# Setting places in each engine's order for the operand steps of the second MLP, and moving three conversion pieces and the last norm

## The chip, the cores and the metric

The kernel runs on one core of a Trainium2 chip. The metric is the device time of one execution in microseconds (us); the median of three runs is used. Engines: TensorE (PE; PEld is its weight load), VectorE (DVE), ScalarE (ACT), GpSimd (POOL) and SyncE (SP), whose queue issues the DMAs.

## The reference

```python
attn_out = _attn_ref(q, k, v)          # 4 x 8 heads, 576 tokens, head size 64: scores * decay mask, @ v
x = attn_out.transpose(0, 2, 1, 3).reshape(2304, 512)
h = x @ w_in                           # 512 -> 2048
x = (h * np.cos(h)) @ w_out            # 2048 -> 512
rms = np.sqrt(np.mean(x * x, axis=-1, keepdims=True) + 1e-06)
xn = x / rms * rms_g
g = xn @ w_gate                        # 512 -> 1536
out = (g / (1 + np.exp(-g)) * (xn @ w_val)) @ w_out   # 1536 -> 512
```

All inputs are float32. The kernel splits operands into a high part and a remainder (`hi`, `lo`) and makes each product of three matmuls: hi·hi, hi·lo, lo·hi.

## The kernel before, in words

**Tokens.** `xall` holds the 2304 tokens (features on the partitions, four chunks of 128). The first MLP goes over five token tiles in the order `ORDER_A = [0, 1, 2, 4, 3]`: four of 512 tokens, and tile 4, of 256, as the fourth. The second MLP goes over three groups of 768 tokens, each as two halves of 384.

**First MLP (stage one).** There are 80 steps `i`, 16 per tile: steps 0 to 15 are tile 0, 48 to 63 the short tile 4, 64 to 79 tile 3, the last. A step makes one block of 128 hidden features (`hidden`, L176 to L178, 12 matmuls into a PSUM tile `g`, of which there are three), then `gate_cos`: ScalarE rounds (L386), VectorE subtracts (L387), ScalarE takes the sine (L389), VectorE multiplies (L393), ScalarE casts to `ghi` (L395), and VectorE or GpSimd makes `glo` (`minus`, L113). Three steps later (`LAG`) `out_t` multiplies the result with the output weights into four accumulators (12 matmuls). At a tile's end ScalarE copies the accumulators to `xall` (L572) and `norm` puts the tile's RMS norm on a list, `background`: four squares, `total` (a cast and a GpSimd `minus`), two pauses, `mean` (two matmuls with ones), two pauses, `guess` (two operations), nine Newton operations, four scales, and a note that the tile is normal: 25 entries. `idle()` takes one entry off; a step calls it once, from step 64 on three times.

The weights of the second MLP are converted beside this in 36 pieces. `piece_steps` weaves one piece into a step's gate: an absolute value on ScalarE, two operations on VectorE, then a cast and a subtraction of the piece before (for output weights only), and three more operations. `begins` lists the steps that begin one: 15 in each of tiles 1 and 2, and six in the short tile, at 48, 50, 53, 56, 58 and 61 (`LAST_BEGINS = (0, 2, 5)`, modulo 8). In steps that begin one, `glo` is made on VectorE, in others on GpSimd.

From step 67 on, `ahead(n)` makes the operands of group 0 one place per step (L522 casts, L526 differences t1 to t4), then, at n = 8 and 10, all of `quad_steps(0)` and `quad_steps(1)`, and fetches three blocks of output weights.

**Second MLP (stage two).** A quad is a pair of weight blocks times one group: seven products (L688, six matmuls of 384 columns each) in two PSUM tiles `alpha` and `beta` from the ring `h` (two slots), combined by ScalarE copies `s` (L695) and VectorE additions (L708, L715, L716) into four results r11, r22, r12, r21. In even quads a result passes through Silu (L710); in odd ones it is multiplied with it and split again (`shi`, `slo`). Between the products stand `fill` matmuls of the output product (L664, nine at a time). There are 12 quads per group, n = 0 to 35. In group 0 `quad_steps(q + 1)` makes the next quad's operands: `step0` (`plain`: a cast L479 and a subtraction), `step1` (four operations on `z`, L483 to L486), `step2` (two casts L491, two subtractions, then two stores by SyncE and the fetch of later values); groups 1 and 2 fetch what was stored. `operand_steps(g + 1)` makes the seven operands of the next group during quads 8 to 11. Three hooks in a quad call these: after r11, before r22's second part, and after r21.

**What sets the order.** From step 16 on ScalarE, VectorE and GpSimd run in the order of the code (`manual_schedule`); in stage two TensorE as well. In stage one TensorE's order is set by the framework's planner.

Of the kernel before, what the change touches and what calls it, by code (L numbers as in the profile page):

```python
# [30 lines left out]
P = 128  # L31
# [33 lines left out]
LAG = 3  # L65
LAST_BEGINS = (0, 2, 5)
MANUAL = NF1
# [8 lines left out]
def body(ctx: ExitStack, tc, qkv, qkr, vr, w1, w2, rg, gq, gk, mask, out):  # L76
# [230 lines left out]
    def norm(t):  # L307
# [20 lines left out]

        def pause():
            pass  # L330

        def mean():
# [26 lines left out]
        background.append(total)  # L359
        background.extend([pause, pause, mean, pause, pause, guess])  # L360
        background.extend([lambda s=s: newton(s) for _ in range(3) for s in range(3)])
        background.extend([lambda kc=kc: scale(kc) for kc in range(KC)])
        background.append(lambda: normal.append(t))

    def idle():
        if background:
            background.pop(0)()

# [75 lines left out]
    begins = [i for i in range(NF1, 3 * NF1) if (i + 1) % NF1]  # L444
    begins += [i for i in range(3 * NF1, 4 * NF1) if i % 8 in LAST_BEGINS]

# [26 lines left out]
    def quad_steps(q):  # L473

        plain, sums = side(q)
        z = values_of.pop(q)

        def step0():
            nc.scalar.copy(plain[:, 0], z[:, :3])  # L479
            minus(nc.vector, plain[:, 1], plain[:, 0], z[:, :3])  # L480

        def step1():
            nc.vector.tensor_tensor(z[:, 4], z[:, 0], z[:, 3], op=ALU.subtract)  # L483
            nc.vector.tensor_tensor(z[:, 3], z[:, 3], z[:, 2], op=ALU.add)
            nc.vector.tensor_tensor(z[:, 0], z[:, 3], z[:, 0], op=ALU.subtract)
            nc.vector.tensor_tensor(z[:, 1], z[:, 1], z[:, 0], op=ALU.subtract)  # L486

        def step2():
            for n in (0, 2):
                src = z[:, n + n // 2:n + n // 2 + 2]  # L490
                nc.scalar.copy(sums[:, 0, n:n + 2], src)  # L491
                minus(nc.vector, sums[:, 1, n:n + 2], sums[:, 0, n:n + 2], src)
# [5 lines left out]
        return [step0, step1, step2]  # L498

# [11 lines left out]
    def operand_steps(g):  # L511

        x = lambda a, b: xall[:, 2 * a:2 * a + 2, g * GROUP + b * HALF:g * GROUP + (b + 1) * HALF]

        def place(k):
            t = places.pop(0) if g else slot()
            ops[g, k] = t, t[:, 0, :, :HALF], t[:, 1, :, :HALF]
            return ops[g, k][1:]

        def split(k, src):  # L520
            hi, lo = place(k)
            nc.scalar.copy(hi, src)  # L522
            minus(nc.vector, lo, hi, src)

        def minus_to(dst, a, b):
            nc.vector.tensor_tensor(dst, a, b, op=ALU.subtract)  # L526

        def t24():
            minus_to(x(1, 1), x(1, 1), x(0, 0))
            split(2, x(1, 1))  # L530
            minus_to(x(1, 0), x(1, 0), x(1, 1))

        def t13():
            minus_to(x(0, 0), x(0, 1), x(0, 0))
            minus_to(x(0, 1), x(1, 1), x(0, 1))

        return [lambda: split(0, x(0, 0)), lambda: split(1, x(1, 0)), t13, lambda: split(5, x(1, 1)), t24,
                lambda: split(3, x(0, 1)), lambda: split(4, x(0, 0)), lambda: split(6, x(1, 0))]

    def ahead(n):  # L540

        if n == 0:
            late["steps"] = operand_steps(0)
        while late["steps"] and len(slots) == n:
            late["steps"].pop(0)()
        if 7 <= n < 11:
            slot()
            if n % 2 == 0:
                a, b = (t.rearrange("p a b c -> p (a b c)") for t in slots[-2:])
                sides.append((a[:, :6 * 2 * P].rearrange("p (h n c) -> p h n c", h=2, n=3),  # L550
                              b.rearrange("p (h n c) -> p h n c", h=2, n=4)))
                for step in quad_steps(len(sides) - 1):
                    step()
        elif n >= 11:
            fetch_out(n - 11)
# [23 lines left out]
    for i in range(LAST + LAG):  # L579
# [28 lines left out]
        if first:  # L608
            while converted[0] < min(len(blocks1), i + CONV_LEAD + 1):
                blocks1[converted[0]].convert(temps())  # L610
                converted[0] += 1
        idle()
        if i >= LAST - NF1:
            idle()
            idle()
        if i >= LAST - NF1 + LAG and len(slots) < NSLOT_A:
            ahead(len(slots))
        if i == MANUAL - 1:
# [7 lines left out]
            order.enter_context(tc.manual_schedule(engines=ENGINES))  # L626
        if i == LAST - NF1 - 1:
            assert len(begins) == npiece and not valued
# [15 lines left out]

    late["mean"] = lambda: acc_tile(5)
    bx = pool("bx", 2)
# [28 lines left out]

    def quad(g, q, fill, hooks):

# [47 lines left out]
        product(alpha, plain[:, :, 0], 0, True)  # L725
        s1 = keep("s1")
        product(beta, plain[:, :, 1], 1, True)
        r11 = result(0, 0, s1, beta)
        next(r11)
        product(alpha, sums[:, :, 0], 2, False)  # L730
        s2 = keep("s2")
        next(r11)
        hooks[0]()
        product(beta, sums[:, :, 3], 3, True)
        product(alpha, sums[:, :, 2], 4, False)
        s4 = keep("s4")
        r22 = result(1, 1, s4, beta)
        next(r22)
        hooks[1]()
        next(r22)  # L740
        fills(9)
        product(alpha, sums[:, :, 1], 5, False)
# [4 lines left out]
        r21 = result(1, 0, s2, beta)  # L747
        next(r21)
        next(r21)
        hooks[2]()  # L750
        fills(9 if q % 2 == 0 else 36)

    fill = []
    todo = []
    for n in range(NGROUP * NQUAD):
        g, q = divmod(n, NQUAD)
        made = []
        if n + 1 < NGROUP * NQUAD and n:
            if g == 0 and q + 1 < NQUAD:
                made = quad_steps(q + 1)  # L760
            else:
                fetch_quad((q + 1) % NQUAD)
        if q == NQUAD - 4 and g + 1 < NGROUP:
            todo = operand_steps(g + 1)
        end = q == NQUAD - 1

        def run(steps, count):
            for _ in range(count):
                if steps:
                    steps.pop(0)()  # L770

        def hook0():
            if end:
                run(todo, 1)
            elif n < 2:
                idle()
                idle()

        def hook1():
            run(made, 2)  # L780
            if end:
                run(todo, 1)
            elif n < 12:
                idle()
                idle()

        def hook2():
            run(made, 1)
            if end:
                run(todo, 3)  # L790
            elif q >= NQUAD - 4:
                run(todo, 1)
            elif n < 12:
                idle()
                idle()

        quad(g, q, fill, (hook0, hook1, hook2))
        if q % 2:
# [5 lines left out]
    for step in fill:  # L804
        step()
    assert not background and not todo
    early.close()
# [59 lines left out]
```

## Time and profile before

| | |
|---|---|
| median of 3 runs | 971.03 us (970.13 to 972.43) |
| profiled execution | 972.07 us, span 970.3 us |
| TensorE busy | 921.6 us, 95% |
| VectorE, ScalarE, GpSimd busy | 616.1, 461.7, 67.4 us |
| mean granted TensorE clock | 0.977 |

Stage one ends at about 516 us in the span; the group changes of stage two lie at about 672 and 817 us. Times are counted from the span's start. In a row of the timeline the square bracket says how long the engine was idle before the instruction and what ended the idle time.

### The profile page before, as it was taken

The numbers are of one execution on the slowest core, as the hardware profiler recorded it, in microseconds if no ns is written. First come the engines' busy times: TensorE is split into PE (matmuls) and PEld (weight loads), VectorE is DVE, ScalarE is ACT, GpSimd is POOL, SyncE is SP. The second block draws the span as 40 slices with busy tenths as digits, with TensorE's granted clock in tenths as the row PEclk, the third lists the DMA queues.
The fourth block names the chain that finished last, engine by engine and source line by source line (L and its number), as shares of the span: only waits on it lengthen the run. The fifth ranks groups of instructions, "written<-read, shape, count | busy, mean of one in ns | idle before, by whom it ended". The sixth has DMA issues, their size and how long they took to land.

```text
span 970.3 us, 12939 instructions
## 1 busy us (share of the span) xinstructions
PE 921.6 (95%) x4996; PEld 806.1 (83%) x4996; DVE 616.1 (63%) x991; ACT 461.7 (48%) x815; POOL 67.4 (7%) x58
## 2 busy tenths in 40 slices
PE   7989999999999999889988889998999998999998
PEld 6777888888878889868767778887999997999997
DVE  3999989788888876748764766667333336333332
ACT  3656575676575665553445334444433333432332
POOL 2321100000000011122221000000000000000000
PEclk8999999999999999889999899999999999999999
DMA  9946361134524542110052366657565555665541
GB/s 330 394 164 218 147 239 44 65 130 152 185 99 152 185 142 76 58 41 1 0 203 123 130 219 236 236 210 271 186 245 216 199 195 196 218 238 195 196 151 66
DMA packets 34733, 163.72 MB, mean 169 GB/s; under 512 B 4080, under 2 KB 5232, under 8 KB 23792
## 3 DMA queue, kind: packets, MB, share of 16 engines
q1 hardware_dynamic: 34672, 162.91, 46.4%
q8 instruction: 39, 0.64, 0.3%
q14 instruction: 22, 0.18, 0.1%
HBM read 123.57 MB, written 39.32 MB: 168 GB/s over the span
## 4 chain that ended last, share of the span: by engine, by line
PE 58%; DVE 24%; ACT 9%; DMA 4%; issue 4%; SPq 0%; POOL 0%; ACTq 0%; DVEq 0%; POOLq 0%
PE h L688 24%; PE acc L664 13%; PE g L176 3%; PE acc L177 3%; PE acc L176 3%; PE g L177 3%; PE acc L178 3%; PE g L178 3%; DVE r L393 3%; DVE w L113 2%; DMA raw<-w_dram 2%; DVE r L387 2%; DVE t L131 2%; ACT r L389 2%; ACT ghi L395 1%
## 5 line engine op out<-in xcount | busy, mean ns | idle before, releaser
L688 PE MATMUL h<-w 128*128 128x384 f32 x1224 | 239.7, 346 | 18.1 <-ACT s L695 11.6
L688 PEld LDWEIGHTS h<-w 128*128 128x128 f32 x1224 | 222.2, 194 | 28.9 <-ACT s L695 14.9
L664 PE MATMUL acc<-w,shi 128*128 128x512 f32 x432 | 134.3, 392 | 0.0
L176 PE MATMUL acc<-ghi,w 128*128 128x512 f32 (+1 forms) x320 | 120.0, 376 | 8.4 <-ACT xall L572 5.8
L176 PE MATMUL g<-xhi,w 128*128 128x512 f32 (+1 forms) x320 | 120.0, 376 | 0.6 <-ACT w L148 0.6
L177 PE MATMUL acc<-glo,w 128*128 128x512 f32 (+1 forms) x320 | 119.6, 374 | 0.7 <-POOL glo L113 0.6
L178 PE MATMUL g<-xhi,w 128*128 128x512 f32 (+1 forms) x320 | 119.1, 372 | 1.2 <-DVE w L113 1.2
L177 PE MATMUL g<-xlo,w 128*128 128x512 f32 (+1 forms) x320 | 119.3, 373 | 0.0
L178 PE MATMUL acc<-ghi,w 128*128 128x512 f32 (+1 forms) x320 | 119.2, 372 | 0.0
L695 ACT COPY s<-h 128x384 f32<-128x384 f32 x108 | 51.6, 478 | 137.5 <-PE h L688 137.5
L708 DVE TENSOR_TENSOR sg<-s,h 128x384 f32<-128x384 f32 x54 | 29.9, 553 | 111.6 <-ACT s L695 59.4
L389 ACT ACTIVATE r<-r,half_pi 128x512 f32<-128x512 f32 (+1 forms) x80 | 54.5, 681 | 78.1 <-DVE r L387 78.0
L664 PEld LDWEIGHTS acc<-w,shi 128*128 128x128 f32 x432 | 80.2, 188 | 13.4
L664 PE MATMUL acc<-w,slo 128*128 128x512 f32 x216 | 85.4, 395 | 0.0
L176 PEld LDWEIGHTS acc<-ghi,w 128*128 128x128 f32 x320 | 61.0, 191 | 19.9 <-ACT xall L572 6.9
L720 ACT CAST shi<-v 128x384 fp32r<-128x384 f32 x72 | 37.1, 515 | 84.7 <-DVE v L716 84.6
L178 PEld LDWEIGHTS g<-xhi,w 128*128 128x128 f32 x320 | 61.2, 191 | 11.9 <-DVE w L113 1.6
L177 PEld LDWEIGHTS acc<-glo,w 128*128 128x128 f32 x320 | 61.3, 192 | 11.5 <-POOL glo L113 1.3
L176 PEld LDWEIGHTS g<-xhi,w 128*128 128x128 f32 x320 | 61.1, 191 | 11.7 <-ACT w L148 0.8
L395 ACT CAST ghi<-r 128x512 fp32r<-128x512 f32 (+1 forms) x80 | 46.2, 578 | 51.6 <-DVE r L393 50.1
L178 PEld LDWEIGHTS acc<-ghi,w 128*128 128x128 f32 x320 | 61.3, 192 | 10.3
L177 PEld LDWEIGHTS g<-xlo,w 128*128 128x128 f32 x320 | 61.1, 191 | 10.1 <-DVE xlo L113 0.2
(86 smaller groups left out, 1307.3 us busy)
## 6 DMA issues: line engine op xcount, KB each, us to landing
w<-s SPq DMA_DIRECT2D x24, 1024.0 KB, 4.8
raw<-w_dram SPq DMA_DIRECT2D x36, 512.0 KB, 4.0
w<-w SPq DMA_DIRECT2D x18, 1024.0 KB, 4.9
w<-s SPq DMA_DIRECT2D x24, 768.0 KB, 6.3
raw<-w_dram SPq DMA_DIRECT2D x16, 1024.0 KB, 7.4
x<-qkv_dram SPq DMA_DIRECT2D x15, 1024.0 KB, 9.4
s<-w SPq DMA_DIRECT2D x12, 1024.0 KB, 4.8
s<-w SPq DMA_DIRECT2D x12, 768.0 KB, 3.2
```

Of the source, the lines that this page charges most:

```text
L113: eng.tensor_tensor(dst, src, hi.bitcast(F32), op=ALU.subtract)
L176: nc.tensor.matmul(dst, a[0], b[0], start=start, stop=False)
L177: nc.tensor.matmul(dst, a[0], b[1], start=False, stop=False)
L178: nc.tensor.matmul(dst, a[1], b[0], start=False, stop=stop)
L389: nc.scalar.activation(r, r, AF.Sin, bias=half_pi, scale=1.0)
L393: nc.vector.tensor_tensor(r, ps, r, op=ALU.mult)
L395: nc.scalar.copy(hi, r)
L664: nc.tensor.matmul(acc, (hi, hi, lo)[k][:, c], w[:, u, (0, 1, 0)[k], :], start=start and u == 0 and k == 0, stop=stop and u == 1 and k == 2)
L688: nc.tensor.matmul(bank, a[:, wp], xp[:, c], start=start and kc == 0 and n == 0, stop=kc == 1 and n == 2, skip_group_check=True)
L695: nc.scalar.copy(t, alpha)
L708: nc.vector.tensor_tensor(t, s, bank, op=ALU.add)
L720: nc.scalar.copy(hi, t)
```

## The change

The six late pieces begin at steps 48, 51, 54, 65, 66 and 67. The fetch of the first values moves from step 63 to step 68. `None` entries take the place of pauses: a call of `idle` stops at one; a norm has 23 entries. In `ahead` all steps up to the next cast run at once, so that differences come a step earlier. In stage two `hooks` become named places (`s1`, `m11`, `r11`, `s4`, `m22`, `r22`, `m21`, `end`): of `quad_steps`, `high0` and `low0` stand at `r11`, `sums0` at `m22`, `high1` at `r22`, `low1` at `m21`, and the stores and the fetch at `end`; the operand steps, with casts and subtractions apart, are spread over quads 8 to 11 and the first quad of the next group. The last norm (tile 3, tokens of group 2 alone) runs four entries at a time at the end of quads 1 to 10 of group 1; its `mean` takes a slot of `h` in place of an accumulator.

```diff
-LAST_BEGINS = (0, 2, 5)
+LAST_BEGINS = [48, 51, 54, 65, 66, 67]
...
-        background.extend([pause, pause, mean, pause, pause, guess])
+        background.extend([None, mean, None, guess] if t != ORDER_A[-1] else [None, mean, guess])
...
-    def idle():
-        if background:
-            background.pop(0)()
+    def idle(count=1):
+
+        for _ in range(count):
+            if background and not background[0]:
+                background.pop(0)
+                break
+            if background:
+                background.pop(0)()
...
-    begins += [i for i in range(3 * NF1, 4 * NF1) if i % 8 in LAST_BEGINS]
+    begins += LAST_BEGINS
...
+        return {"r11": [high0, low0], "m22": [sums0], "r22": [high1], "m21": [low1], "end": [keep]}
...
+        return (split(0, x(0, 0)) + split(1, x(1, 0)) + t1 + t3 + split(5, x(1, 1)) + t2 + split(2, x(1, 1)) + t4
+                + split(3, x(0, 1)) + split(4, x(0, 0)) + split(6, x(1, 0)))
...
-        while late["steps"] and len(slots) == n:
+        while late["steps"] and (len(slots) == n or late["steps"][0].__name__ != "high"):
...
-        idle()
-        if i >= LAST - NF1:
-            idle()
-            idle()
+        if i // NF1 != 3 or 1 not in normal:
+            idle(3 if i >= LAST - NF1 else 1)
...
-        if i == LAST - NF1 - 1:
+        if i == LAST_BEGINS[-1] + 1:
...
-    late["mean"] = lambda: acc_tile(5)
+    late["mean"] = lambda: psp.tile([P, 512], F32, tag="h", bufs=2, name="h")
...
+    spread = {NQUAD - 4: {"end": 2}, NQUAD - 3: {"end": 2}, NQUAD - 2: {"end": 2},
+              NQUAD - 1: {"s1": 1, "m11": 2, "s4": 1, "m22": 2, "r22": 1, "end": 2}, 0: {"s1": 1, "m11": 1, "m22": 1}}
...
+            s = operand_steps(g + 1)
+            hi3, lo3, hi4, lo4, hi6, lo6 = s[-6:]
+            tokens = s[:-6] + [hi3, lo3, hi4, hi6, lo4, lo6]
+        if tokens and q in spread:
+            for where, count in spread[q].items():
+                more[where] = more.get(where, []) + [tokens.pop(0) for _ in range(count)]
+        if g == 1 and 0 < q < NQUAD - 1:
+            more["end"] = more.get("end", []) + [lambda: idle(4)]
```

## Rows read from the trace of the kernel before

**Rows 1.** Page, part 1: busy us, share of the span, instructions.
```profile
PE 921.6 (95%) x4996; PEld 806.1 (83%) x4996; DVE 616.1 (63%) x991; ACT 461.7 (48%) x815; POOL 67.4 (7%) x58
```
**Rows 2.** Windows: busy us of PE, PEld, DVE, ACT, POOL; PEclk, DMA share, GB/s.
```profile
682.00:816.00 134.00, 133.93 (x696) 124.16 (x695) 50.94 (x88) 44.74 (x90) 0.00 (x0) 1.00 0.57 210
```
**Rows 3.** Waits of PE, 400 to 516 us: total us, times, longest.
```profile
PE acc L176 <- ACT xall L572: 4.1, 1, 4.1
PE acc L176 <- ACT ghi L395: 2.6, 1, 2.6
PE g L335 <- ACT nt L325: 2.3, 1, 2.3
```
**Rows 4.** Waits of PE, 516 to 970 us.
```profile
PE h L688 <- ACT s L695: 14.0, 10, 2.6
PE h L688 <- DVE v L716: 4.3, 2, 3.7
PE h L688 <- DVE v L715: 1.4, 4, 0.6
```
**Rows 5.** Timeline of DVE, short tile: start us, us, instruction [idle before].
```profile
381.27 0.42 DVE L387 SCALAR_TENSOR_TENSOR r<-r,g 128x256 f32<-128x256 int32 x1 [0.30 <-ACT r L386]
...
383.60 0.42 DVE L387 SCALAR_TENSOR_TENSOR r<-r,g 128x256 f32<-128x256 int32 x1 [0.30 <-ACT r L386]
...
387.69 0.68 DVE L352 SCALAR_TENSOR_TENSOR nt<-nt 128x512 f32<-128x512 f32 x1
388.29 0.41 DVE L387 SCALAR_TENSOR_TENSOR r<-r,g 128x256 f32<-128x256 int32 x1
...
397.40 1.23 DVE L352 SCALAR_TENSOR_TENSOR nt<-nt 128x512 f32<-128x512 f32 x1
```
**Rows 6.** Timeline of POOL, short tile.
```profile
397.28 0.80 POOL L113 TENSOR_TENSOR glo<-r,ghi 128x256 fp32r<-128x256 f32 x1 [6.21 <-ACT ghi L395]
```
**Rows 7.** Timeline of DVE: L387 in tile 2 (first two) and tile 3.
```profile
339.81 0.68 DVE L387 SCALAR_TENSOR_TENSOR r<-r,g 128x512 f32<-128x512 int32 x1
...
345.36 0.68 DVE L387 SCALAR_TENSOR_TENSOR r<-r,g 128x512 f32<-128x512 int32 x1
...
416.17 0.69 DVE L387 SCALAR_TENSOR_TENSOR r<-r,g 128x512 f32<-128x512 int32 x1 [2.88 <-ACT r L386]
...
438.79 0.69 DVE L387 SCALAR_TENSOR_TENSOR r<-r,g 128x512 f32<-128x512 int32 x1 [0.33 <-ACT r L386]
...
444.23 0.69 DVE L387 SCALAR_TENSOR_TENSOR r<-r,g 128x512 f32<-128x512 int32 x1 [0.17 <-ACT r L386]
...
452.07 0.68 DVE L387 SCALAR_TENSOR_TENSOR r<-r,g 128x512 f32<-128x512 int32 x1
...
483.31 0.68 DVE L387 SCALAR_TENSOR_TENSOR r<-r,g 128x512 f32<-128x512 int32 x1
...
492.54 0.68 DVE L387 SCALAR_TENSOR_TENSOR r<-r,g 128x512 f32<-128x512 int32 x1
...
496.03 0.69 DVE L387 SCALAR_TENSOR_TENSOR r<-r,g 128x512 f32<-128x512 int32 x1 [1.33 <-ACT r L386]
...
508.80 0.69 DVE L387 SCALAR_TENSOR_TENSOR r<-r,g 128x512 f32<-128x512 int32 x1
```
**Rows 8.** Timeline of PE, products of stage two after a wait.
```profile
623.77 3.41 PE L688 MATMUL h<-w 128*128 128x384 f32 x18 [1.10 <-ACT s L695]
...
648.90 4.96 PE L688 MATMUL h<-w 128*128 128x384 f32 x18 [1.83 <-ACT s L695]
...
677.42 4.81 PE L688 MATMUL h<-w 128*128 128x384 f32 x18 [2.37 <-ACT s L695]
```
**Rows 9.** Timeline of ACT: casts ahead of `s1`, quad 5's end and the group's start.
```profile
597.81 1.14 ACT L491 CAST w<-z 128x512 fp32r<-128x512 f32 x2
...
674.70 2.29 ACT L522 CAST w<-xall 128x768 fp32r<-128x768 f32 x3
```
**Rows 10.** Timeline of ACT, first quad of stage two.
```profile
523.84 0.62 ACT L325 CAST nt<-nt 128x512 fp32r<-128x512 f32 x1 [0.76 <-DVE nt L320]
```

More of the change, by code (lines that the diff above doesn't have):

```diff
@@ L476, in quad_steps, with high0, low0, sums0 @@
         z = values_of.pop(q)
-        def step0():
+        def high0():
             nc.scalar.copy(plain[:, 0], z[:, :3])
+        def low0():
             minus(nc.vector, plain[:, 1], plain[:, 0], z[:, :3])
-        def step1():
+        def sums0():
             nc.vector.tensor_tensor(z[:, 4], z[:, 0], z[:, 3], op=ALU.subtract)
@@ L486, in step1, with high1, low1, keep @@
             nc.vector.tensor_tensor(z[:, 1], z[:, 1], z[:, 0], op=ALU.subtract)
[L488 to L492, printed above, removed]
+        src = [z[:, 0:2], z[:, 3:5]]
+        def high1():
+            for n in range(2):
+                nc.scalar.copy(sums[:, 0, 2 * n:2 * n + 2], src[n])
+        def low1():
+            for n in range(2):
+                minus(nc.vector, sums[:, 1, 2 * n:2 * n + 2], sums[:, 0, 2 * n:2 * n + 2], src[n])
+        def keep():
             for part, where in zip((plain, sums), kept[q]):
@@ L496, in step2 @@
                 fetch_values(q + 2)
-        return [step0, step1, step2]
+        return {"r11": [high0, low0], "m22": [sums0], "r22": [high1], "m21": [low1], "end": [keep]}
     kept = [[dram.tile([P, 2, n, 2 * P], F32, tag=f"s{n}_{q}", name=f"s{n}_{q}") for n in (3, 4)] for q in range(NQUAD)]
@@ L520, in split, with high, low, difference @@
         def split(k, src):
[L521 to L538, printed above, removed]
+            def high():
+                hi, _ = place(k)
+                nc.scalar.copy(hi, src)
+            def low():
+                _, hi, lo = ops[g, k]
+                minus(nc.vector, lo, hi, src)
+            return [high, low]
+        def difference(dst, a, b):
+            return [lambda: nc.vector.tensor_tensor(dst, a, b, op=ALU.subtract)]
+        t1 = difference(x(0, 0), x(0, 1), x(0, 0))
+        t3 = difference(x(0, 1), x(1, 1), x(0, 1))
+        t2 = difference(x(1, 1), x(1, 1), x(0, 0))
+        t4 = difference(x(1, 0), x(1, 0), x(1, 1))
+        return (split(0, x(0, 0)) + split(1, x(1, 0)) + t1 + t3 + split(5, x(1, 1)) + t2 + split(2, x(1, 1)) + t4
+                + split(3, x(0, 1)) + split(4, x(0, 0)) + split(6, x(1, 0)))
     def ahead(n):
         if n == 0:
+            assert {0, 1} <= set(normal)
             late["steps"] = operand_steps(0)
-        while late["steps"] and len(slots) == n:
+        while late["steps"] and (len(slots) == n or late["steps"][0].__name__ != "high"):
             late["steps"].pop(0)()
@@ L551, in ahead @@
                               b.rearrange("p (h n c) -> p h n c", h=2, n=4)))
-                for step in quad_steps(len(sides) - 1):
-                    step()
+                for step in quad_steps(len(sides) - 1).values():
+                    for part in step:
+                        part()
         elif n >= 11:
@@ L674, in body, with quad, also @@
     silus = {}
-    def quad(g, q, fill, hooks):
+    def quad(g, q, fill, more):
+        def also(where):
+            for step in more.get(where, ()):
+                step()
         val = q % 2
@@ L726, in quad @@
         s1 = keep("s1")
+        also("s1")
         product(beta, plain[:, :, 1], 1, True)
@@ L729, in quad @@
         next(r11)
+        also("m11")
         product(alpha, sums[:, :, 0], 2, False)
@@ L732, in quad @@
         next(r11)
-        hooks[0]()
+        also("r11")
         product(beta, sums[:, :, 3], 3, True)
@@ L736, in quad @@
         s4 = keep("s4")
+        also("s4")
         r22 = result(1, 1, s4, beta)
         next(r22)
-        hooks[1]()
+        also("m22")
         next(r22)
+        also("r22")
         fills(9)
@@ L748, in quad @@
         next(r21)
+        also("m21")
         next(r21)
-        hooks[2]()
         fills(9 if q % 2 == 0 else 36)
+        also("end")
     fill = []
-    todo = []
+    tokens = []
+    spread = {NQUAD - 4: {"end": 2}, NQUAD - 3: {"end": 2}, NQUAD - 2: {"end": 2},
+              NQUAD - 1: {"s1": 1, "m11": 2, "s4": 1, "m22": 2, "r22": 1, "end": 2}, 0: {"s1": 1, "m11": 1, "m22": 1}}
     for n in range(NGROUP * NQUAD):
         g, q = divmod(n, NQUAD)
-        made = []
+        more = {}
         if n + 1 < NGROUP * NQUAD and n:
             if g == 0 and q + 1 < NQUAD:
-                made = quad_steps(q + 1)
+                more = quad_steps(q + 1)
             else:
@@ L763, in body @@
         if q == NQUAD - 4 and g + 1 < NGROUP:
[L764 to L797, printed above, removed]
+            assert len(normal) == (4, 5)[g]
+            s = operand_steps(g + 1)
[6 more added lines that the diff above has]
+            more["end"] = more.get("end", []) + [lambda: idle(4)]
+        quad(g, q, fill, more)
         if q % 2:
@@ L805, in body @@
         step()
-    assert not background and not todo
+    assert not background and not tokens
     early.close()
```

2 lines of the change are left out of this document (removed).

## The prediction

> **What bounds the kernel now.** The page comes first: TensorE is busy 95% of the span [rows 1], so what can be won is its idle time and its slow clock. The windows by stage come next. In group 1 of the second MLP TensorE is busy 133.93 of 134 us at full clock [rows 2], so this stage has nothing to give, only to lose. Then the waits of TensorE in two stretches. From 400 to 516 us (end of the short tile, whole last tile) it waits 4.1 us for the copies that empty the accumulators, 2.6 for a cast `ghi`, and 2.3 for the cast behind the norm's `mean`, whose second matmul waits about as long again [rows 3]. After 516 us it waits 14.0 us in ten places for ScalarE's copy `s` and 4.3 in two for VectorE's `v` [rows 4]. Last, the timelines of the engines named: who stands in front of these steps in their queues?
>
> A long wait costs twice. After a wait of 1.10 us, 18 matmuls took 3.41 us; after 1.83 and 2.37 us the same 18 took 4.96 and 4.81 [rows 8], so I count 1.55 us (4.96 - 3.41) of slow clock for each stop of that kind.
>
> **Fewer pieces in the short tile.** In this tile the gate chain of a step runs ScalarE, VectorE, ScalarE, VectorE, ScalarE. From one L387 to the next it takes 2.33 us where only one norm operation goes along and 4.69 where a piece is begun [rows 5]; TensorE needs about 2.7 (an estimate: half of the 5.44 from 438.79 to 444.23, where the last tile runs at TensorE's pace [rows 7], since this tile has half the columns). So a step with a piece puts the chain 2 us behind and one without gains back 0.4. Before, six begin there, the last three in the second half, and the chain ends up behind: these are the waits of 2.6 and 4.1. After, three begin, the last at step 54, with nine steps to recover in. The chain loses 3 × 2.36 = 7.1 us; TensorE sets the pace at the end, so I let the last tile's first L387 (416.17) come 6.4 earlier.
>
> **The same three pieces in the last tile** (steps 65 to 67, the finishing cast and subtraction at 68). Before, the chain from 416.17 to 508.80 is fifteen steps in 92.6 us [rows 7], where TensorE needs 15 × 5.44 = 81.6: this tile is set by the chain, not by TensorE. I walk the new order with the old prices [rows 7]: a step with a piece and one addition 5.55 (339.81 to 345.36); a bare step 3.5 (492.54 to 496.03); one with three norm operations and operand work 7.84 (444.23 to 452.07); one with a whole `quad_steps` 9.23 (483.31 to 492.54). In us for steps 64 to 78: 5.45, 7.05 (piece, addition, the total's cast ahead of the next gate), 5.35, 8.6 (piece, guess, newton, first operand), 8.5 (t1 and t3 now come here), 6.9, 7.0, 5.5, 5.0, 5.3, 3.5, 9.25, 3.5, 9.25, 3.5. Sum 93.65, one more than before. So 6.4 - 1.0 = 5.4 us are left. One thing takes some back: the short tile's `mean` moves from step 76 to 74, one step behind its total as before, but now the chain is further behind and a light step follows. While TensorE stands at `mean` it does not make the next gate's input; I price this at 2.0. **Stage one gains 3.4 us.** Bounds: +10 if both large waits and their slow clock go and nothing comes back; -4 if a second stop like that at `mean`, with its slow clock, is not hidden.
>
> Where no piece is begun, the gate's `lo` is made on GpSimd and not on VectorE: so it is now in steps 50, 53, 56, 58 and 61, and no longer in 51, 54 and 65 to 67. A newton operation beside a GpSimd subtraction took 1.23 us, without one 0.68 [rows 5, 6]. Five such meetings at 0.55 are 2.75 us in the short tile, less than the nine steps' recovery of 3.6: nothing in the sum. The Trainium skill ("SBUF — State Buffer", Who interferes with whom) goes further: a VectorE operation with two SBUF inputs and a GpSimd operation that reads SBUF block each other, and the later one waits until the first is finished. By that rule five meetings could cost the whole 0.80 of the subtraction [rows 6] each, 4.0 us, 0.4 more than is recovered, and the sum below would be 951.9. The row, at 0.55, has the operation wait for a part only.
>
> The fetch of the first two quads' values moves from step 63 to 68 and its use stays at 75, seven steps of over 5 us: free. If it were late, `quad_steps(0)` would wait at the head of both queues.
>
> **Second MLP, group 0.** (a) The last norm leaves. In the first quad the copy `s` for product 4 stands behind a square and the total's cast, which itself waits for VectorE [rows 10]; without them `s` follows the Silu, and the longest wait, 2.6, falls to 0.9 (the table load stays). In the second quad the norm's guess and two newton operations, some 2.5 us at 0.68 each [rows 5], stand ahead of the multiply that frees `alpha`: the 3.7 wait [rows 4] falls to 1.9. (b) `low0` goes ahead of `s4`, where VectorE idles; `high1` goes ahead of r12's cast. Before, both casts of `sums` (1.14) are issued between r21's cast and the next quad's `s1` [rows 9]. After, `s1` follows r21's cast directly; the wait of 1.1 at the ends of quads 5 and 7 [rows 8] falls to 0.3. (c) Quads 8 to 11: the next group's operands are cut in halves and spread. Before, three casts in a row (2.29) hold `s1` at the group's start [rows 9]; after, one (0.84, an estimate: a third of that with its overlap). That wait of 2.4, at both group changes, falls to 0.75; the 1.83 at the end of quad 9 to 0.5.
> The ten waits for `s` thus fall from 14.0 to 0.5 + 0.9 + 0.6 + 0.3 + 0.3 + 0.5 + 0.75 + 0.75 = 4.6 (two vanish): 9.4 gained. Those for `v` of L716 fall from 4.3 to 1.9: 2.4; those for L715 from 1.4 to 0.6: 0.8. Slow clock after four stops (fourth quad, quad 9, both group changes) 6.2. Together 18.8. The DMAs of `keep` stay behind the quad's work and ahead of the fetch of `wout`, so SyncE's order is the same. What is late next: VectorE's r11 addition at the group changes, about where `s1` now ends.
>
> **Second MLP, group 1.** The last norm's remaining seventeen steps come here, up to four at a quad's end. They stand on ScalarE and VectorE ahead of the next quad's `s1` and r11. At quad 1 a square, an addition and a cast make `s1` 0.9 late; at 3 four newton operations (2.8) make r11's addition 1.35 late; at 5 three scales 0.65 late: 2.9 lost where nothing was lost [rows 2]. At even quads the queue is empty enough. `mean` takes a slot of `h`; the nine matmuls of fill before it cover its wait. Bounds: 1 to 8 (three stops with slow clock).
> **Stage two gains 18.8 - 2.9 = 15.9**, bounds 9 (half of the waits return at the next instruction in the queue) and 22.
>
> **Sum.** The profiled execution took 972.07 us. 972.07 - 3.4 - 15.9 = 952.8; it stands 1.0 above the median of the runs shown, 971.03, so I forecast **951.5**.
>
> **Rivals.**
> A. The last tile takes all back: TensorE's order in stage one is the planner's, and it may put `mean` early in a chain further behind. For it: 92.6 against 81.6 [rows 7]. Stage one gains 0 to -4: 955 to 959. Chance 0.18.
> B. Stage one gives more: `mean` is hidden and pieces fit where VectorE idled before. 4 to 7 us more: 945 to 947; with the upper bound of stage two 940. Chance 0.15.
> C. Waits in group 0 are only shifted by one instruction, or the norm brings slow clock to group 1. Half of stage two: 958 to 963. Against it: no instruction is added in group 0, and the norm's 21 leave. Chance 0.13.
> D. Slower. In group 0 `high1` now stands in ScalarE's queue ahead of r12's cast, and waits for the four operations of `sums0`; `high0` stands ahead of `s4`. If either is late in each of the ten quads that are made there, each next `s1` is late too. At 2.4 of wait and 1.5 of slow clock, as at the group's start [rows 4, 8], ten quads pay 39 us, less 19: 991. It decides from 1.9 us a quad on. Against it: the same four operations stood ahead of r12's multiply before, and the casts `shi` are not among what TensorE waits for [rows 4]. Chance 0.05.
> E. The change does not act: the pieces or steps fall on the same places in the queues. The lists differ in the code, so only for single parts: counted in A and C; a net of nothing 0.02.
>
> **How the numbers follow.** Forecast (947 to 956) 0.47, A 0.18, B 0.15, C 0.13, D 0.05, E 0.02. What a measurement here can tell from no change is about 0.2%, 2 us. Range 940 to 962: B's lower end to C's, with D and E and a little of C outside. Faster 0.93, same 0.02, slower 0.05.
>
> **What would show it.** Right: the wait for `ghi` gone at the end of the short tile, for `xall` under 3 us; the first L387 of the last tile 5 to 7 earlier; a wait at `mean` still there; waits for `s` after 516 us about 5 us; at the group changes under 1 us and full clock; three waits of about 1 us in group 1. Wrong: TensorE's wait in the last tile above 10 us, new waits for `shi` or `s` at every quad of group 0, or a clock below full in group 1.

## The result, and the profile after

The changed kernel takes 943.46 us (median of 4, 940.8 to 944.31) against 971.01 (970.13 to 972.43): ratio 0.971, 95% interval 0.9687 to 0.9733. The forecast was 951.5, its range 940 to 962. The profiled execution took 940.8 us, the shortest of the four, with a span of 939.0; before it was 972.07 with 970.3 [rows 1]. The two profiles differ by 31.3 us, the two medians by 27.6: what is counted by stages below is the difference of the profiles.

Page of the changed kernel, part 1:

```profile
PE 908.7 (97%) x4996; PEld 797.0 (85%) x4996; DVE 612.3 (65%) x991; ACT 462.6 (49%) x815; POOL 62.3 (7%) x58
```

The instructions are the same in number; TensorE's busy time fell by 12.9 us, its idle time by 18.4 (the rest of the 31.3). Line numbers have shifted: L387 is now L389, L395 L397, L688 L703, L695 L710, L715 and L716 L730 and L731, L335 L332, L352 L349. L716 is the multiplication that makes `v`, not one of the additions, among which the description of the kernel before counts it. Quads are counted from 0 in each group.

All profiles below are cut at the same places: the rounding subtraction (L387, now L389) of steps 40, 64 and 79, and the first product of each group. The first 40 steps differ only in the pauses of two norms (313.01 us before, 312.75 after), and the time to get there varies by itself (last section), so stages are compared from step 40.

| us | before | after | gain |
|---|---|---|---|
| steps 40 to 64 (end of tile 2, short tile) | 103.16 | 92.82 | 10.3 |
| steps 64 to 79 (last tile's chain) | 92.63 | 97.25 | -4.6 |
| step 79 to the first quad | 7.25 | 6.54 | 0.7 |
| group 0 | 156.06 | 136.95 | 19.1 |
| group 1 | 143.16 | 142.47 | 0.7 |
| group 2 to the end | 155.00 | 150.21 | 4.8 |
| sum | 657.25 | 626.25 | 31.0 |

So stage one gave 6.4 where 3.4 was forecast, stage two 24.6 where 15.9 was.

Timeline of VectorE after, the last tile's first and last subtraction (start, us, instruction, idle before):

```profile
405.58 0.69 DVE L389 SCALAR_TENSOR_TENSOR r<-r,g 128x512 f32<-128x512 int32 x1 [1.18 <-ACT r L388]
...
502.83 0.69 DVE L389 SCALAR_TENSOR_TENSOR r<-r,g 128x512 f32<-128x512 int32 x1
```

They stood at 416.17 and 508.80 [rows 7]: the tile begins 10.6 earlier and ends 6.0 earlier. TensorE's waits after, 400 to 512 us (total, times, longest):

```profile
PE g L332 <- ACT nt L325: 3.6, 2, 3.3
PE acc L176 <- ACT ghi L397: 3.1, 2, 1.7
PE acc L177 <- POOL glo L113: 2.8, 4, 0.9
PE g L333 <- POOL nt L113: 0.4, 1, 0.4
```

The wait of 4.1 for `xall` [rows 3] is gone. In its place stands a stop of 3.3 at tile 2's `mean`; smaller ones for `ghi` and `glo` stand around the short tile's `mean`, where they sum to 3.5, and at the end of the last tile. Windows of the changed kernel around the two (busy us of PE, PEld, DVE, ACT, POOL; PEclk, DMA share, GB/s):

```profile
416.00:423.00 7.00, 5.51 (x17) 4.21 (x18) 4.82 (x9) 5.10 (x11) 1.28 (x1) 0.76 0.11 40
...
470.00:477.00 7.00, 5.86 (x17) 4.40 (x18) 2.98 (x4) 3.22 (x6) 2.35 (x3) 0.76 0.00 0
```

After each of them part of TensorE's work ran at the lower of its two levels.

TensorE's waits after 509 us:

```profile
PE h L703 <- ACT s L710: 3.2, 4, 1.4
PE h L703 <- DVE v L731: 1.5, 1, 1.5
PE h L703 <- DVE sg L723: 1.1, 2, 1.0
PE h L703 <- DVE v L730: 0.4, 1, 0.4
```

Against [rows 4], `s` fell from 14.0 to 3.2, of which 1.4 is new in group 1, and `v` of the multiplication (L716, now L731) from 4.3 to 1.5. Windows by group (0, 1, 2 to the last product), first of the kernel before, then after:

```profile
516.05:672.11 156.06, 140.59 (x688) 126.63 (x686) 99.05 (x176) 64.27 (x125) 1.28 (x1) 0.96 0.53 189
672.11:815.27 143.16, 140.43 (x721) 130.01 (x721) 56.03 (x95) 48.73 (x98) 0.00 (x0) 0.99 0.57 210
815.27:966.64 151.37, 148.70 (x756) 136.64 (x756) 50.95 (x91) 49.73 (x100) 0.00 (x0) 0.99 0.50 182
```

```profile
509.36:646.32 136.96, 133.22 (x686) 123.04 (x684) 89.54 (x163) 64.89 (x124) 0.00 (x0) 0.99 0.59 217
646.32:788.79 142.47, 139.82 (x723) 128.74 (x722) 66.11 (x112) 50.07 (x99) 1.28 (x1) 1.00 0.57 211
788.79:935.40 146.61, 146.57 (x757) 135.08 (x755) 49.80 (x89) 48.51 (x98) 0.00 (x0) 1.00 0.52 188
```

First column against second: TensorE's idle time in stage two fell from 20.9 to 6.4 us, 14.4 less; its busy time for the same matmuls fell by 10.1. Of this 8.5 is slow clock that no longer comes: by the granted clock, the lower level cost TensorE 10.2 us in stage two before, at five places, and 1.7 after, at one. What makes the other 1.6 is not shown. The longest of the five, before, lies behind the wait of 3.7 for `v` [rows 4] in quad 2 of group 0; the one that is left, after, lies behind the wait of 1.5 at the same place:

```profile
540.00:548.00 8.00, 7.74 (x26) 6.30 (x25) 5.15 (x9) 2.93 (x7) 0.00 (x0) 0.57 0.40 130
```

```profile
528.00:536.00 8.00, 7.30 (x31) 6.98 (x32) 4.38 (x9) 3.43 (x7) 0.00 (x0) 0.79 0.41 132
```

Group change, ScalarE and TensorE after:

```profile
646.87 0.51 ACT L735 CAST shi<-v 128x384 fp32r<-128x384 f32 x1 [1.68 <-DVE v L731]
647.28 0.83 ACT L533 CAST w<-xall 128x768 fp32r<-128x768 f32 x1
648.02 0.47 ACT L710 COPY s<-h 128x384 f32<-128x384 f32 x1
```

```profile
648.54 3.40 PE L703 MATMUL h<-w 128*128 128x384 f32 x18
...
673.25 3.42 PE L703 MATMUL h<-w 128*128 128x384 f32 x18 [1.42 <-ACT s L710]
```

One cast of 0.83 stands ahead of `s1`, not three of 2.29 [rows 9]; the 18 matmuls follow without a wait, in 3.40, not 4.81 [rows 8]. The second row is the new stop in group 1, and ScalarE shows what stands ahead of its `s1`: two output copies, then the norm's square and cast.

```profile
669.84 1.06 ACT L679 COPY o<-acc 128x512 f32<-128x512 f32 x2
670.80 0.64 ACT L316 ACTIVATE nt<-xall 128x512 f32<-128x512 f32 x1
672.20 0.62 ACT L325 CAST nt<-nt 128x512 fp32r<-128x512 f32 x1 [0.76 <-DVE nt L320]
672.72 0.47 ACT L710 COPY s<-h 128x384 f32<-128x384 f32 x1
```

### The profile page after: what moved, and what is told of

Read it like the earlier page. It is cut to its first block, busy times and chain, and to the rows that moved or that the text cites. A ratio compares the mean times of both kernels' runs of the same rounds, so it can differ in the third digit from the quotient of the medians.

```text
span 939.0 us, 12936 instructions
## 1 busy us (share of the span) xinstructions
PE 908.7 (97%) x4996; PEld 797.0 (85%) x4996; DVE 612.3 (65%) x991; ACT 462.6 (49%) x815; POOL 62.3 (7%) x58
## 4 chain that ended last, share of the span: by engine, by line
PE 72%; DVE 18%; ACT 5%; issue 3%; DMA 1%; SPq 0%; POOL 0%; ACTq 0%; DVEq 0%; POOLq 0%
PE h L703 26%; PE acc L675 15%; PE g L176 4%; PE g L177 4%; PE g L178 4%; PE acc L177 4%; PE acc L178 4%; PE acc L176 4%; DVE w L113 2%; DVE r L395 2%; DVE r L389 2%; DVE t L131 2%; PE g L270 1%; DVE t L132 1%; ACT r L391 1%
## 5 line engine op out<-in xcount | busy, mean ns | idle before, releaser
L703 PE MATMUL h<-w 128*128 128x384 f32 x1224 | 231.1, 339 | 6.4 <-ACT s L710 3.2
L703 PEld LDWEIGHTS h<-w 128*128 128x128 f32 x1224 | 216.4, 189 | 14.2 <-ACT s L710 5.2
L176 PE MATMUL acc<-ghi,w 128*128 128x512 f32 (+1 forms) x320 | 118.2, 372 | 4.2 <-ACT ghi L397 3.1
L178 PE MATMUL acc<-ghi,w 128*128 128x512 f32 (+1 forms) x320 | 118.0, 369 | 0.0
L710 ACT COPY s<-h 128x384 f32<-128x384 f32 x108 | 51.7, 479 | 129.5 <-PE h L703 129.5
L397 ACT CAST ghi<-r 128x512 fp32r<-128x512 f32 (+1 forms) x80 | 46.2, 578 | 50.8 <-DVE r L395 47.6
L177 PEld LDWEIGHTS g<-xlo,w 128*128 128x128 f32 x320 | 61.1, 191 | 10.1
```

The costliest lines, as they stand in the source:

```text
L176: nc.tensor.matmul(dst, a[0], b[0], start=start, stop=False)
L177: nc.tensor.matmul(dst, a[0], b[1], start=False, stop=False)
L178: nc.tensor.matmul(dst, a[1], b[0], start=False, stop=stop)
L397: nc.scalar.copy(hi, r)
L703: nc.tensor.matmul(bank, a[:, wp], xp[:, c], start=start and kc == 0 and n == 0, stop=kc == 1 and n == 2, skip_group_check=True)
L710: nc.scalar.copy(t, alpha)
```

## The experiments

Four kernels undo one part each of the changed kernel, one does a part alone on the kernel before, and six go further. Diffs are against the changed kernel where nothing else is said. Stage times are of single profiles, cut as above; a ratio is to the kernel before on the same chip.

**Pieces back in the short tile.**

```diff
-LAST_BEGINS = [48, 51, 54, 65, 66, 67]
+LAST_BEGINS = [48, 50, 53, 56, 58, 61]
```

> The changed kernel, but the six late pieces begin again at 48, 50, 53, 56, 58 and 61 of the short tile; all else as changed. Theory (the gate chain sets the last tile, and its start is what was won): the first L389 of the last tile comes back to 413 to 417, the waits for ghi and xall at the tile's end return, and the last tile's own chain gets 3 to 6 us shorter, so 947 to 951. Rival (the pieces only change places, the chain loses in the last tile what it won in the short one): within 2 us of 943.5.

Measured: 949.11 us, 0.9763 (0.9736 to 0.979). Steps 40 to 64 take 100.15 us (+7.3), the last tile's chain 94.95 (-2.3), the way to the first quad 0.4 more: 5.5 in stage one, nothing after. TensorE's waits from 400 to 516 us:

```profile
PE g L332 <- ACT nt L325: 9.5, 2, 4.9
PE acc L176 <- ACT ghi L397: 2.5, 1, 2.5
```

The wait for `ghi` is back at 2.5 (2.6 in [rows 3]): the short tile ends behind again. The wait for `xall`, also expected, is not back; TensorE stands 4.9 us at tile 2's `mean` and 4.6 at the short tile's. The last tile's chain gets 2.3 shorter, not 3 to 6. Beside the other edits the pieces take 7.3 us out of the short tile and put 2.3 of it into the last.

**Pieces alone**, on the kernel before.

```diff
-LAST_BEGINS = (0, 2, 5)
+LAST_BEGINS = [48, 51, 54, 65, 66, 67]
...
-    begins += [i for i in range(3 * NF1, 4 * NF1) if i % 8 in LAST_BEGINS]
+    begins += LAST_BEGINS
...
-        if i == LAST - NF1 - 1:
+        if i == LAST_BEGINS[-1] + 1:
```

> The kernel before, with the new places of the six late pieces and of the first values' fetch alone. Theory (as for the changed kernel: the last tile's chain starts 8 to 11 us earlier and takes 3 to 6 us longer): 964 to 967, the waits of 2.6 for ghi and 4.1 for xall gone. Rival (the gain of this part needs the earlier norm of tile 1 and the earlier differences): 969 to 971.

Measured: 961.3 us (959.06 to 967.77), 0.9916 (0.9889 to 0.9942). Stage one from step 40: 194.49 against 203.03, 8.5 gained, 3.0 more than undoing says. Steps 40 to 64 take 93.38, the chain 94.27. So the pieces alone give 9.8 of the 10.3 by which the last tile begins earlier and make its chain 1.6 longer; the other edits of stage one (the `None` stops, the differences a step earlier) make it 3.0 longer still, and with them stage one takes 196.61. The profile is of one of the shorter of its ten executions (959.38). The wait for `ghi` is gone, as expected, but most of the one for `xall` is not (TensorE's waits, 400 to 515 us):

```profile
PE g L335 <- ACT nt L325: 4.4, 1, 4.4
PE acc L176 <- ACT xall L572: 3.1, 1, 3.1
```

So the wait for `xall` is not the pieces'. In every kernel here TensorE stops once early in the last tile: at tile 2's `mean` (3.3 to 4.9 us) where that `mean` comes early, for `xall` (0.9 to 5.3) where it does not.

Group 0, whose code is untouched here, is 3.7 shorter too, most of it in quads 4 and 10 (1.54 and 1.53). Timeline of TensorE in quad 10, the window over it, and the same window of the kernel before:

```profile
637.88 3.44 PE L688 MATMUL h<-w 128*128 128x384 f32 x18 [1.83 <-ACT s L695]
```

```profile
633.80:648.80 15.00, 13.17 (x69) 11.98 (x68) 9.78 (x18) 7.31 (x15) 0.00 (x0) 1.00 0.63 238
```

```profile
644.82:659.82 15.00, 13.17 (x61) 12.10 (x60) 8.26 (x16) 6.84 (x14) 0.00 (x0) 0.89 0.55 200
```

The wait is the 1.83 of [rows 8] to the last digit, but the 18 matmuls take 3.44 at full clock, not 4.96. The same stop costs slow clock in one execution and none in another.

**Last norm back in group 0.**

```diff
-    late["mean"] = lambda: psp.tile([P, 512], F32, tag="h", bufs=2, name="h")
+    late["mean"] = lambda: acc_tile(5)
...
-        if g == 1 and 0 < q < NQUAD - 1:
-            more["end"] = more.get("end", []) + [lambda: idle(4)]
+        for where in ("r11", "m22", "end"):
+            if n < 12 and (n < 2 or where != "r11"):
+                more[where] = more.get(where, []) + [lambda: idle(2)]
```

The norm's pauses stand as before.

> The changed kernel, but the last norm runs in group 0 as before (two entries at r11 and m22 in the first two quads, two at each quad's m22 and end, its mean in an accumulator). Theory (the norm's operations stand ahead of what frees alpha and beta): the first five quads get 7 to 10 us longer, group 1 gets its 4 us back, 946 to 950. Rival (the new order of the quad steps alone opens the first quads): 939 to 942, since group 1 wins and group 0 loses nothing.

Measured: 944.73 us, 0.9733 (0.9699 to 0.9766). Group 0 takes 144.42 us (+7.5), group 1 138.38 (-4.1), all its quads after the first at 11.5: the move is worth 3.3 us, by the medians 1.3. In quad 1 the norm's operations hold up `v` again, and TensorE waits at the start of quad 2:

```profile
533.59 4.98 PE L704 MATMUL h<-w 128*128 128x384 f32 x18 [3.24 <-DVE v L732]
```

**The next quad's steps back** at two places, in the old order.

```diff
-        return {"r11": [high0, low0], "m22": [sums0], "r22": [high1], "m21": [low1], "end": [keep]}
+        return {"m22": [high0, low0, sums0], "e21": [both1, keep]}
```

`both1` casts and subtracts in turn; `e21` comes right after r21.

> The changed kernel, but the quad steps stand where they stood: plain's cast and subtraction and the four operations at m22, both casts and subtractions of sums after r21. Theory (the two casts hold the next quad's s1): waits for s of about 1.1 us return at the ends of quads 5, 7 and 9 and 2 to 4 us in quads 1 to 4; 948 to 952. Rival (the norm was what made those casts late): only the 1.1 us at quads 5, 7 and 9, 946 to 947.

Measured: 951.64 us, 0.9798 (0.9775 to 0.9822). Group 0 +8.3, and +2.4 in stage one, where the first two quads' steps run. Quads 4, 6 and 8 take 12.9 (11.5 after), quad 10 15.17 (12.14). Waits of TensorE after 510 us:

```profile
PE h L708 <- ACT s L715: 8.6, 9, 1.8
```

Five more waits for `s`: both casts are issued in one go ahead of the next `s1`. The longest, 1.8 in quad 10, is the one of [rows 8].

**The next group's operand steps back.**

```diff
-    spread = {NQUAD - 4: {"end": 2}, NQUAD - 3: {"end": 2}, NQUAD - 2: {"end": 2},
-              NQUAD - 1: {"s1": 1, "m11": 2, "s4": 1, "m22": 2, "r22": 1, "end": 2}, 0: {"s1": 1, "m11": 1, "m22": 1}}
+    spread = {NQUAD - 4: {"e21": 2}, NQUAD - 3: {"e21": 2}, NQUAD - 2: {"e21": 2},
+              NQUAD - 1: {"r11": 2, "m22": 4, "e21": 6}}
```

> The changed kernel, but the next group's operand steps stand where they stood: whole casts and subtractions after r21 of quads 8 to 10, then at r11, m22 and after r21 of quad 11, three casts in a row ahead of the next group's s1. Theory (queue in front of s1, and slow clock after the wait): a wait of 2.4 us and 1.5 of slow clock at each group change, 951 to 954. Rival (the quad steps' casts made that wait): under 1 us at each change, 944 to 946.

Measured: 951.86 us, 0.9801 (0.9777 to 0.9824); groups 1 and 2 are 5.2 and 4.8 longer, at their first quads: 16.67 and 16.38 against 11.73. ScalarE and TensorE at the first change:

```profile
649.82 2.29 ACT L533 CAST w<-xall 128x768 fp32r<-128x768 f32 x3
652.02 0.47 ACT L710 COPY s<-h 128x384 f32<-128x384 f32 x1
```

```profile
652.54 5.27 PE L703 MATMUL h<-w 128*128 128x384 f32 x18 [2.37 <-ACT s L710]
```

The row of before returns: three casts of 2.29, a wait of 2.37, 18 matmuls on slow clock. Quad 10 of group 0 stays at 12.11, so the operand steps alone do not make its wait of before.

From step 40, undoing costs 5.7 (pieces), 3.3 (norm), 10.9 (quad steps) and 10.7 (operand steps): 30.6 of the 31.0. **The parts add up** to the whole, by stage less closely: 8.2 against 6.4 in stage one, where the edits that none of the four undoes cost something, and 16.1 against 19.1 in group 0.

**`mean` one step later**, for all tiles but the last.

```diff
-        background.extend([None, mean, None, guess] if t != ORDER_A[-1] else [None, mean, guess])
+        background.extend([None, None, mean, None, guess] if t != ORDER_A[-1] else [None, mean, guess])
```

> The changed kernel with one more None ahead of the mean, so that in the last tile each mean's matmuls stand a step later behind their total. Theory (the chain of ScalarE and VectorE sets the last tile; a stop of TensorE at a mean is slack spent early): the waits at both means go, others at glo, ghi or xall take their place, the chain from its first to its last L389 stays at 95 to 98 us, 942 to 945. Rival (the stops at the means are lost time): 3 to 6 us less, 937 to 940.

Measured: 936.75 us, 0.9661 (0.9631 to 0.9691). TensorE's waits from 400 to 512 us:

```profile
PE g L176 <- DVE r L395: 4.7, 1, 4.7
PE g L332 <- ACT nt L325: 1.2, 1, 1.2
```

The stop of 3.3 at tile 2's `mean` is gone; the 1.2 is at the short tile's, where it was 0.2. The chain falls from 97.25 to 93.48; later TensorE waits 4.7 on the chain itself, for the multiplication on VectorE (L395). Stage one is 2.5 shorter, group 0 1.7 (quad 0 8.35, not 9.12), group 1 0.7 longer. Of the 5.6 between the two profiles the way to step 40 makes 2.3, so the 6.7 between the medians is not all this edit's (last section). Stage one now takes 194.10, about what it takes with the pieces alone (194.49): so the earlier `mean` accounts for about what the other edits cost there. That the chain alone sets the last tile, so that stops of TensorE in it cost nothing, does not hold.

**The last norm in the even quads of group 1**, inside the quad, without the `None` in its list.

```diff
+    norms = {2: {"r11": 1, "r22": 1, "end": 2}, 4: {"r11": 3, "r22": 3, "m21": 3}, 6: {"r11": 2, "r22": 2, "end": 1}}
...
-        if g == 1 and 0 < q < NQUAD - 1:
-            more["end"] = more.get("end", []) + [lambda: idle(4)]
+        for where, count in (norms.get(q, {}) if g == 1 else {}).items():
+            more[where] = more.get(where, []) + [lambda count=count: idle(count)]
```

> The changed kernel, but the last norm's entries stand in quads 2, 4 and 6 of group 1, at r11, r22 and m21, where VectorE idles for 3 us, instead of four at a time at each quad's end. Theory (what group 1 lost was queue in front of s1 and r11): quads 2 to 6 of group 1 come back to 11.5 us but for the 0.45 of mean, 939 to 941. Rival (the operations cost the same wherever they stand): 943 to 944.

Measured: 936.95 us, 0.9656 (0.9623 to 0.9688). Group 1 takes 138.73, as without any norm (138.38): moving the same operations gives back 3.7 of the 4.1.

**The short tile's norm goes there as well**, out of the last tile: both are put on a list `held`, which group 1 takes.

```diff
-        background.extend([lambda kc=kc: square(kc) for kc in range(KC)])
+        todo = background if t in ORDER_A[:3] else held
+        todo.extend([lambda kc=kc: square(kc) for kc in range(KC)])
...
+    norms = {0: {"r22": 5, "end": 2}, 2: {"r11": 4, "r22": 5, "m21": 5}, 4: {"r11": 2, "r22": 3, "end": 2},
+             6: {"r11": 3, "r22": 3, "m21": 3}, 8: {"r11": 5}}
```

> The changed kernel, but the norm of the short tile, which group 2 alone needs, leaves the last tile as well: both last norms run in the even quads of group 1. Theory (the chain of ScalarE and VectorE, not TensorE, sets the last tile): the chain from its first to its last L389 falls from 97 to 88 to 91 us, stage one ends 6 to 9 us earlier, and group 1 stays at 11.5 us a quad: 931 to 935. Rival (the wait at the mean and the pace of TensorE set it): 938 to 942.

Measured: 938.71 us, 0.9671 (0.9636 to 0.9706). Stage one gains 1.1 only: the chain takes 94.07 (97.25), but the way to the first quad 8.59 (6.54), and TensorE waits 4.4 for one `ghi`. Less work on the chain alone does not shorten the tile. Group 1 takes 141.20, 2.5 more than with one norm.

**A piece less in the last tile**, and two entries of the norm a step there in place of three: as the kernel above, with

```diff
-LAST_BEGINS = [48, 51, 54, 65, 66, 67]
+LAST_BEGINS = [48, 51, 54, 58, 65, 66]
...
-            idle(3 if i >= LAST - NF1 else 1)
+            idle(2 if i >= LAST - NF1 else 1)
```

> As the kernel with both norms in group 1, and in the last tile two entries of tile 2's norm a step instead of three, and one more piece in the short tile (48, 51, 54, 58, 65, 66). Theory (the short tile recovers 0.5 us a step after a piece, so a fourth one at 58 is recovered by 62; fewer operations at 67 to 71 let the chain keep TensorE's pace): another 2 to 4 us, 928 to 932. Rival (a fourth piece leaves the chain behind at the end of the short tile): not under 933.

Measured: 936.42 us, 0.9643 (0.9601 to 0.9685). Steps 40 to 64 take 94.63 (+1.8 against the changed kernel), the chain 88.79 (-8.5): stage one 190.43, 6.2 less. Which of the two edits does it is not taken apart. The time is above the 928 to 932 that was expected, and group 1 still takes 143.00. ScalarE there:

```profile
648.37 1.32 ACT L316 ACTIVATE nt<-xall 128x256 f32<-128x256 f32 x4
...
656.09 0.58 ACT L680 COPY o<-acc 128x512 f32<-128x512 f32 x1 [3.29 <-DMA out_dram<-o]
656.57 0.49 ACT L711 COPY s<-h 128x384 f32<-128x384 f32 x1
```

Four squares in quad 0 make the output copies late; a later copy then waits 3.29 us for a store that has not left its buffer, and `s` stands behind it, for which TensorE waits 1.8. ScalarE's queue is held by a DMA.

**The norms from quad 2 on**, where the first output copies are done.

```diff
-    norms = {0: {"r22": 5, "end": 2}, 2: {"r11": 4, "r22": 5, "m21": 5}, 4: {"r11": 2, "r22": 3, "end": 2},
-             6: {"r11": 3, "r22": 3, "m21": 3}, 8: {"r11": 5}}
+    norms = {2: {"r11": 2, "r22": 3, "end": 2}, 4: {"r11": 4, "r22": 5, "m21": 5}, 6: {"r11": 2, "r22": 3, "end": 2},
+             8: {"r11": 5, "r22": 6, "m21": 3}}
```

> As the kernel with a piece at 58 and both norms in group 1, but the norms stand in quads 2, 4, 6 and 8 and none in quad 0. Theory (in quad 0 the squares held the copies of the output tiles, whose stores then came too late for the third copy and so for s1): quad 1 of group 1 comes back from 15.1 to 11.5, group 1 loses only the two means' 0.9 us, 931 to 934. Rival (wherever two norms stand, group 1 loses 3 us): 935 to 937.

Measured: **931.87 us** (930.85 to 932.4), 0.9594 (0.9573 to 0.9616), the fastest of all. Windows of groups 0 and 1:

```profile
505.78:641.07 135.29, 131.83 (x686) 121.53 (x684) 88.18 (x161) 63.41 (x121) 0.00 (x0) 1.00 0.59 219
641.07:780.20 139.13, 139.13 (x725) 129.13 (x724) 74.69 (x132) 52.91 (x107) 2.03 (x2) 1.00 0.59 216
```

In group 1 TensorE is busy 139.13 of 139.13 us with two norms beside it, and quad 1 is back at 11.5 (15.07 in the kernel above).

**Five pieces up to the end of the short tile**: as the kernel above, with `LAST_BEGINS = [48, 51, 54, 57, 60, 65]`.

> As the kernel before it, with five pieces in the short tile (48, 51, 54, 57, 60) and one at 65. Theory (every third step a piece leaves the chain 0.7 us further behind, still within what three PSUM tiles allow; the last tile's chain gets 2 us shorter and starts 1 to 2 later): within 1 us of the four-piece kernel, 930 to 934. Rival (the short tile's end stops TensorE again, with slow clock): 935 to 938.

Measured: 932.99 us, 0.9615 (0.9591 to 0.9639): no better. Steps 40 to 64 take 98.00 (94.62), the chain 88.37 (88.92). The fifth piece costs the short tile 3.4 and saves the last 0.6.

## Why the prediction was right, and where its sizes failed

**Fewer pieces: right in kind, too small.** The last tile's start was to come 6.4 us earlier; it came 10.3, counted from step 40, and the pieces alone give 9.8 (7.3 when they are undone beside the other edits). The sum had the lost chain time, 7.1, but not the slow clock behind the wait for `ghi`, which only the upper bound of +10 had. Before, the clock there was 0.57:

```profile
407.00:415.00 8.00, 7.01 (x22) 5.73 (x23) 5.66 (x9) 3.81 (x9) 1.78 (x2) 0.57 0.50 199
```

After, and with the pieces alone, no lower level was granted at the short tile's end. The prediction also puts the wait of 4.1 for `xall` down to the pieces; the kernel with the pieces alone, where 3.1 of it stays, shows that this is not so.

The five meetings of a newton operation with GpSimd's subtraction, feared as 2.75 us in the short tile, did not show in its bare steps (timelines of VectorE and GpSimd after):

```profile
373.18 0.68 DVE L349 SCALAR_TENSOR_TENSOR nt<-nt 128x512 f32<-128x512 f32 x1
```

```profile
373.90 0.74 POOL L113 TENSOR_TENSOR glo<-r,ghi 128x256 fp32r<-128x256 f32 x1 [8.56 <-ACT ghi L397]
```

The newton operation ends at 373.86, `ghi` at 373.76, the subtraction starts at 373.90: they follow each other, and each newton operation takes its 0.68. So the rule of the Trainium skill ("SBUF — State Buffer", Who interferes with whom) had nothing to act on there, and its 4.0 us fell away with the 2.75. In the last tile they do meet:

```profile
444.05 1.62 POOL L113 TENSOR_TENSOR glo<-r,ghi 128x512 fp32r<-128x512 f32 x1 [6.94 <-ACT ghi L397]
```

```profile
444.56 1.66 DVE L347 SCALAR_TENSOR_TENSOR nt<-nt 128x512 f32<-128x512 f32 x1
```

When the newton operation starts, the subtraction has 1.11 us left, and it takes 0.98 longer than its 0.68. In [rows 5] and [rows 6] 0.68 was left, not the whole 0.80, and it took 0.55 longer. The prediction read from this that the operation waits for a part only; against what was left, it waits for all but 0.13 us in both, and there the trace agrees with that rule.

**The last tile: the walk held but for one place.** Forecast 93.65, measured 97.25. Over twelve of the fifteen steps forecast and trace differ by 0.1 us in sum and by 0.63 at most; steps 72 to 74, around the short tile's `mean`, took 5.88, 6.64 and 4.75 against 5.0, 5.3 and 3.5: 3.5 us, the 2.0 set aside for a stop at that `mean` and 1.5 more. But at that `mean` itself TensorE waits 0.6 us; 3.5 more just before it are for `ghi` and `glo`. Without the short tile's norm in the last tile these waits are gone and the three steps take 13.6, as walked (13.8); which of the norm's operations makes them is not shown. The largest stop, 3.3, is at tile 2's `mean` (417.49), where the sum has none; the steps around it took what the walk gave them. With every `mean` one step later, stage one is 2.5 shorter. Stage one: 6.4, not 3.4.

**Group 0 and the group changes: the step that failed.** "The ten waits for `s` thus fall from 14.0 to ... 4.6": they fell to 1.8 outside group 1's new stop. The three of the first two quads came as forecast (1.8 for 2.0); the five remainders counted behind r21's cast and at the group changes, 2.6 together, are not there: `s1` is issued at 648.02, and the row at 648.54 shows no wait. The wait of 1.83 in quad 10 was put down to the operand steps; it is back at 1.8 with the quad steps put back, and not with the operand steps alone put back: it takes the quad steps' casts. `v` of L716 fell to 1.5 (forecast 1.9), of L715 to 0.4 (0.6). All waits together fell by 14.4, where the sum, less its new waits in group 1, had 9.7; busy time by 10.1, where it had 6.2 of slow clock for four stops. The trace has a fifth: behind the wait for `v` in quad 2, which the sum shortens but gives no slow clock, TensorE lost 3.4 before and 1.7 after. Of the slow clock that went, some 3 us need not be the change's: in the kernel with the pieces alone quads 4 and 10 ran at full clock behind the waits of before.

**Group 1's norm: 4.1, not 2.9.** The copies of the output (1.06) ahead of the square at quad 1's end were left out of the queue: `s1` came 1.42 late, 0.5 more than the 0.9 forecast, and the quad it delays took 13.67 against 11.5 (2.15). The other delays were 1.21 at quad 3 (1.35 forecast) and 0.42 at quad 5 (0.65); `mean` cost 0.34, as good as covered. It could be had for 0.35 (138.73 against 138.38).

**Rivals.** A (the last tile takes all back) has its mechanism in the trace, 4.6 longer, but not its size. B's reason (more from stage one) gave 3.0 more, not 4 to 7; the measured time lies between its 945 and the 940 that it gives with stage two's upper bound. C is refuted by the waits, D by the quads of group 0 at 11.5, E by the four parts, each with its cost when undone. So the time came from the mechanisms named. From step 40 the profiles gained 11.7 more than forecast, 3.0 in stage one and 8.7 in stage two, whose 24.6 lies above its upper bound of 22; the medians missed by 8.0. Most of it is what was left standing in group 0 and at the group changes. That the time still fell inside the range is owed to B's lower end, and part of the excess may be chance (last section).

What stays open: the last tile before was the shorter one (92.63), and why a chain of 94.07 without the short tile's norm falls to 88.79 with one piece less and two entries a step was not walked step by step. In the fastest kernel TensorE still waits 3.7 us for `xall` in the last tile.

## What to carry to other kernels

When background work is placed in an engine's order, look at what stands between it and the next instruction that frees TensorE's accumulator: the same cast costs nothing in the middle of a product and a stop at its end. Count everything in that queue, output copies and the DMA that frees their buffers too. When a chain of steps has both heavy and light ones, put heavy steps where lighter ones follow to recover, and size both stretches together: a piece moved on costs where it lands.

## What was not expected of the hardware

**A stop does not always cost slow clock.** With the same wait of 1.83 us on the same code, 18 matmuls took 4.96 us in one execution (0.89 granted in the 15 us around it) and 3.44 in another (1.00). The prediction counted 1.55 for every long stop; it is a chance, not a price. Thirteen executions of the kernel before, on one chip, took 966.45 us at a mean granted clock of 0.988 to 975.11 at 0.974. The Trainium skill ("TensorE: Matmul & The Clock Gate", Part 1) says of a kernel's start that the number of slow matmuls varies from run to run; here it varies behind a stop in the middle.

**The start varies.** The thirteen profiles reach step 40 at 310.5 to 315.4 us. The code of the two below is the same in the first tile, where nearly all of their difference arises: first the kernel with the last norm in even quads (step 40 at 311.70), then the one with two norms there (315.42):

```profile
0.00:75.00 75.00, 64.15 (x584) 53.40 (x585) 58.90 (x78) 40.59 (x67) 19.09 (x20) 1.00 0.80 301
```

```profile
0.00:75.00 75.00, 64.32 (x559) 53.73 (x560) 56.07 (x73) 39.92 (x67) 17.04 (x20) 0.95 0.77 288
```

In the same 75 us one gets 584 matmul instructions done at a granted clock of 1.00, the other 559 at 0.95. That is why stages are compared from step 40, and why a difference of 1 or 2 us between two medians is not read as an effect.
